# Transposing part of the attention output on VectorE and 16 small DMAs instead of on TensorE

## The chip, the core and the metric

One of the cores of a Trainium2 chip runs the whole kernel. The metric is the device time of one execution in microseconds (us). A profile's span, from its first to its last instruction, is one to three us shorter than that time. Before the change the median was 315.37 us in three runs (314.56 to 315.74).

Engine names in the profile: PE is TensorE (matmul), PEld its weight loads, DVE is VectorE, ACT is ScalarE, POOL is GpSimd, SP is SyncE. POOLq and SPq are the instruction streams of these engines; GpSimd and SyncE mostly issue DMAs here.

## The reference, cut to what matters

```python
def reference(q, k, v, centroids, w_in, w_out, alpha):   # q, k, v: (4, 8, 768, 64)
    # each query and key is assigned to one of 16 clusters of its head;
    # scores are masked to pairs of the same cluster
    attn = softmax(where(mask, q @ k.T / 8, -1e9)) @ v
    x = attn.transpose(0, 2, 1, 3).reshape(4 * 768, 512)
    h = x @ w_in                                         # (3072, 2048)
    g = h + sin(alpha * h) ** 2 / alpha
    return g @ w_out                                     # (3072, 512)
```

## The kernel before: the parts that matter

There are four batches. In each, four pairs of heads go through attention in 48 steps (12 per pair; a step is one tile of 128 keys by 768 queries of one head). Then the hidden matmuls multiply x by `w_in`. They need x with its 512 columns on partitions (`xT`), so each pair's result `xs`, which has queries on partitions, is transposed. In each step PE makes the scores (S<-QK), ScalarE takes their exponential ("exp" below), and PE multiplies that with V (the "PV" matmuls, OB<-VX,pT). The mask comes from one-hot rows, which mark the cluster of each query and key and stand below the 64 rows of q and k in the tile QK; DMAs put them there (QK<-ohT).

```python
    def x_T(m, bk=None):                      # six 128x128 transposes on PE, one copy on DVE
        b, hp = pair_of[m]
        xs = st[m]["xs"]
        xt_ps = (bank() if bk is None else bk).bitcast(BF16)
        for j in range(NJ):
            nc.tensor.transpose(
                out=xt_ps[:, P * j : P * j + P], in_=xs[:, j, :, :], identity=ident_b
            )
        nc.vector.tensor_copy(out=xT[:, hp, :], in_=xt_ps[:, 0:S])

    def hidden_mm(f, ar, k0, k1):
        for kk in range(k0, k1):
            lhsT = w_in_bf[:, kk, P * f : P * f + P]
            for lo, hi in ((0, 512), (512, S)):
                nc.tensor.matmul(..., lhsT=lhsT, rhs=xT[:, kk, lo:hi], ...)
```

The work beside the main chain is put at fixed steps, and each engine takes its own instructions in the order written. GpSimd has, in batches 1 and 2: eight casts of later queries and keys per pair (`prep_cast`), one cast of V per pair (`prep_v`), and the loads of q, k and v.

```python
    def prep_new(m, k0):                      # a later pair: k0 = 48 * b + 12 * n
        for g, d in enumerate((-12, -11, -9, -8)):
            at(k0 + d, lambda g=g: prep_D(m, g))     # DVE transposes of q, k
        at(k0 - 8, lambda: prep_S(m))                # 8 copies T<-Tq, issued by SyncE
        at(k0 + 5, lambda: prep_cast(m, 0))          # GpSimd
        at(k0 + 6, lambda: prep_cast(m, 1))
        hot_steps(m, k0 + 8)                         # one-hot rows of the clusters
    ...
            at(max(0, STEPS * m - (14 if m < 5 else 26)), lambda m=m: load_v(m, nc.gpsimd))
        at(max(0, STEPS * m - 5), lambda m=m: prep_v(m))
    ...
        pv(base + ASTEPS - 2)                 # end of a batch's attention
        hidden_mm(0, A[0], 0, KX - 2)         # x of the first two pairs
        pv(base + ASTEPS - 1)
```

The softmax here doesn't subtract the row's maximum and nothing guards it: scores larger than these inputs give would overflow.

## Time and profile before

| | before |
|---|---|
| median time | 315.37 us |
| span of the profile | 312.8 us |
| PE busy | 304.7 us, 97% |
| first exp of batches 0 to 3, at | 12.02, 84.04, 155.74, 226.97 us |
| attention of batches 0 to 3, first to last exp | 41.72, 41.01, 40.55, 38.56 us |
| first hidden matmul of batches 0 to 3, at | 53.13, 124.57, 195.80, 265.05 us |

The page of the kernel before shows busy time per engine (us, share, instructions), then the span in 40 slices with the busy share in tenths; PEclk is the granted TensorE clock in tenths.

```profile
PE 304.7 (97%) x2786; PEld 181.8 (58%) x2786; DVE 203.8 (65%) x367; ACT 239.9 (77%) x324; POOL 112.7 (36%) x174
...
PE   8899999999999999999999999999999999999995
...
POOL 5889886319307165870005376520001000000000
PEclk9999999999999999999999999999999999999999
```

PE is the limit nearly everywhere, and its clock is full throughout. The timeline of the kernel before (start, duration, engine, line, operation, output<-inputs, count) shows what one pair's transposes cost PE:

```profile
98.34 0.34 PE L340 MATMUL OB<-VX,pT 128*128 128x65 bf16 x6
98.52 0.50 PE L364 MATMUL M<-ident_b,xs 128*128 128x128 bf16 x6
98.86 0.38 PE L372 MATMUL M<-w_out_bf,gT 128*128 128x512 bf16 x1
```

The recorded durations overlap: 0.50 us are recorded for the six transposes, and yet the next matmul starts after 0.34. What counts is the distance between starts: the six hold PE from 98.52 to 98.86, 0.34 us. And the timeline of GpSimd shows DMAs issued one after another:

```profile
125.78 0.72 POOL L117 DMA_DIRECT2D q<-in_q_dram  x1
126.50 0.72 POOL L117 DMA_DIRECT2D k<-in_k_dram  x1
```

A DMA line on POOL is the time to issue it. Its data moves afterwards, and the time from issue to landing stands elsewhere in the profile (2.3 us for a copy T<-Tq).

### The profile page before, as it was taken

The numbers are of one execution on the slowest core, as the hardware profiler recorded it, in microseconds if no ns is written. First come the engines' busy times: TensorE is split into PE (matmuls) and PEld (weight loads), VectorE is DVE, ScalarE is ACT, GpSimd is POOL, SyncE is SP. The second block draws the span as 40 slices with busy tenths as digits, with TensorE's granted clock in tenths as the row PEclk, the third lists the DMA queues.
The fourth block names the chain that finished last, engine by engine and source line by source line (L and its number), as shares of the span: only waits on it lengthen the run. The fifth ranks groups of instructions, "written<-read, shape, count | busy, mean of one in ns | idle before, by whom it ended". The sixth has DMA issues, their size and how long they took to land.

```text
span 312.8 us, 7244 instructions
## 1 busy us (share of the span) xinstructions
PE 304.7 (97%) x2786; PEld 181.8 (58%) x2786; DVE 203.8 (65%) x367; ACT 239.9 (77%) x324; POOL 112.7 (36%) x174
## 2 busy tenths in 40 slices
PE   8899999999999999999999999999999999999995
PEld 3475757455456656555556656555556666555544
DVE  4768687688865867576957767587835222677821
ACT  5588889787689898688679988778678999687300
POOL 5889886319307165870005376520001000000000
PEclk9999999999999999999999999999999999999999
DMA  7576997978553776980044675320011001000031
GB/s 216 162 247 202 298 178 163 191 130 289 179 138 77 162 175 121 279 290 27 0 119 112 153 179 111 110 84 2 0 69 47 36 2 37 0 36 0 0 136 67
DMA packets 27138, 37.74 MB, mean 121 GB/s; under 512 B 4304, under 2 KB 20960, under 8 KB 27104
## 3 DMA queue, kind: packets, MB, share of 16 engines
q0 software_dynamic: 8704, 19.93, 24.3%
q1 hardware_dynamic: 18160, 17.30, 20.6%
q8 instruction: 22, 0.36, 0.5%
q14 instruction: 12, 0.10, 0.1%
q10 hardware_dynamic: 240, 0.06, 0.1%
HBM read 27.30 MB, written 6.29 MB: 107 GB/s over the span
## 4 chain that ended last, share of the span: by engine, by line
PE 86%; DVE 4%; ACT 3%; DMA 3%; POOL 1%; issue 1%; SPq 1%; ACTq 0%; DVEq 0%
PE M L372 19%; PE S L403 17%; PE S L325 12%; PE OB L340 10%; PE M L403 8%; PE S L326 6%; PE OB L372 5%; PE M L213 3%; PE M L143 3%; PE S L372 2%; DVE gT L426 2%; DMA q<-in_q_dram 2%; ACT s_sb L414 1%; PE M L364 1%; DMA QK<-ohT 1%; POOL QK L185 1%
## 5 line engine op out<-in xcount | busy, mean ns | idle before, releaser
L331 ACT ACTIVATE pT<-S 128x768 bf16<-128x768 f32 x192 | 143.9, 810 | 18.9 <-PE S L326 17.7
L372 PE MATMUL M<-w_out_bf,gT 128*128 128x512 bf16 (+1 forms) x288 | 90.7, 373 | 0.2
L325 PE MATMUL S<-QK 80*128 80x512 bf16 x192 | 73.0, 380 | 1.6 <-DMA QK<-ohT 1.1
L403 PEld LDWEIGHTS <-w_in_bf 128*128 128x128 bf16 x512 | 49.4, 98 | 37.7 <-issue 1.8
L340 PEld LDWEIGHTS <-pT 128*128 128x128 bf16 x1152 | 56.0, 97 | 21.3 <-ACT pT L331 0.2
L403 PE MATMUL S<-xT,w_in_bf 128*128 128x512 bf16 x352 | 65.0, 326 | 0.7 <-DVE gT L426 0.6
L340 PE MATMUL OB<-VX,pT 128*128 128x65 bf16 x1152 | 61.2, 193 | 0.0
L190 POOL TENSOR_SCALAR QK<-T 64x384 bf16<-64x384 f32 x64 | 34.4, 538 | 66.7 <-DMA T<-Tq 63.4
L414 ACT ACTIVATE s_sb<-S,alpha_col 128x768 bf16<-128x768 f32 (+2 forms) x45 | 39.4, 886 | 23.1 <-PE S L403 13.9
L372 PEld LDWEIGHTS <-gT 128*128 128x128 bf16 x400 | 39.0, 97 | 30.7 <-issue 5.4
L326 PE MATMUL S<-QK 80*128 80x256 bf16 x192 | 51.9, 270 | 0.0
L426 DVE SCALAR_TENSOR_TENSOR gT<-u_sb,ralpha,S 128x768 bf16<-128x768 bf16 (+2 forms) x45 | 44.7, 996 | 10.4 <-ACT u_sb L419 7.6
L185 POOL CAST QK<-T 64x768 bf16<-64x768 f32 x32 | 26.9, 841 | 9.1 <-DVE T L149 4.7
L403 PE MATMUL M<-xT,w_in_bf 128*128 128x512 bf16 (+1 forms) x160 | 29.9, 326 | 0.0
L326 PEld LDWEIGHTS <-QK 80*128 80x128 bf16 x192 | 18.9, 98 | 16.2 <-issue 2.1
L351 DVE RECIPROCAL rec<-OB 128x6 f32<-128x6 f32 x32 | 6.2, 195 | 33.7 <-PE OB L340 33.7
L422 DVE TENSOR_TENSOR u_sb<-s_sb 128x768 bf16<-128x768 bf16 (+2 forms) x41 | 22.9, 560 | 7.1 <-ACT s_sb L414 7.0
L414 ACT ACTIVATE s_sb<-M,alpha_col 128x512 bf16<-128x512 f32 (+1 forms) x40 | 20.9, 573 | 7.2 <-PE M L403 7.2
L426 DVE SCALAR_TENSOR_TENSOR gT<-u_sb,ralpha,M 128x512 bf16<-128x512 bf16 (+1 forms) x40 | 22.8, 611 | 5.5 <-ACT u_sb L419 5.1
L372 PE MATMUL OB<-w_out_bf,gT 128*128 128x512 bf16 (+1 forms) x80 | 26.2, 358 | 0.2 <-ACT T L153 0.2
L202 POOL CAST VX<-v 128x768 bf16<-128x768 f32 x16 | 13.5, 843 | 34.5 <-PE OB L340 33.4
L325 PEld LDWEIGHTS <-QK 80*128 80x128 bf16 x192 | 18.6, 97 | 8.9 <-issue 5.0
(81 smaller groups left out, 264.4 us busy)
## 6 DMA issues: line engine op xcount, KB each, us to landing
T<-Tq SPq DMA_DIRECT2D x64, 96.0 KB, 2.3
out_dram<-o_sb SPq DMA_DIRECT2D x23, 256.0 KB, 2.1
v<-in_v_dram POOLq DMA_DIRECT2D x14, 384.0 KB, 4.4
q<-in_q_dram POOLq DMA_DIRECT2D x13, 384.0 KB, 5.9
k<-in_k_dram POOLq DMA_DIRECT2D x13, 384.0 KB, 6.3
w_in_bf<-in_moe_w_in_dram POOLq DMA_DIRECT2D x4, 512.0 KB, 6.5
w_out_bf<-in_moe_w_out_dram POOLq DMA_DIRECT2D x4, 512.0 KB, 9.0
QK<-ohT SPq DMA_DIRECT2D x62, 12.0 KB, 4.2
```

What stands on the lines that cost most here:

```text
L185: nc.gpsimd.tensor_copy(out=QK[0:D, m % NQK, h, :, HS * par : HS * par + HS], in_=src)
L190: nc.gpsimd.tensor_scalar(out=QK[0:D, m % NQK, h, t].rearrange("c (n i a) -> c i n a", i=4, a=32)[:, 2 * par : 2 * par + 2], in0=src[:, t] ...
L202: nc.gpsimd.tensor_copy(out=VX[m % NVX][:, :, :, 0:D], in_=st[m]["v32"])
L325: nc.tensor.matmul(out=dst[:, 0:512], lhsT=lhsT, rhs=T[:, 0, 0:512], start=True, stop=True)
L326: nc.tensor.matmul(out=dst[:, 512:S], lhsT=lhsT, rhs=T[:, 0, 512:S], start=True, stop=True)
L331: nc.scalar.activation(out=pT, in_=area(i)[:, 0:S], func=ACTF.Exp, scale=escale)
L340: nc.tensor.matmul(out=o3[:, j, :], lhsT=pT[:, P * j : P * j + P], rhs=VX[m % NVX][:, h, jof(m // NHP, kt), :], start=(kt == 0 and j == 0) ...
L372: nc.tensor.matmul(out=bk[:, lo:hi], lhsT=gT[:, f, P * mt : P * mt + P], rhs=w_out_bf[:, f, lo:hi], start=(f == 0), stop=(f == NF - 1),)
L403: nc.tensor.matmul(out=ar[lo // 512][:, 0 : hi - lo] if isinstance(ar, tuple) else ar[:, lo:hi], lhsT=lhsT, rhs=xT[:, kk, lo:hi], start=(k ...
L414: nc.scalar.activation(out=s_sb[:, lo:hi], in_=src, func=ACTF.Sin, scale=alpha_col[:, f : f + 1])
L422: nc.vector.tensor_tensor(out=u_sb[:, lo:hi], in0=s_sb[:, lo:hi], in1=s_sb[:, lo:hi], op=ALU.mult)
L426: nc.vector.scalar_tensor_tensor(out=gT[:, f, lo:hi], in0=u_sb[:, lo:hi], scalar=ralpha[:, f : f + 1], in1=src, op0=ALU.mult, op1=ALU.add,)
```

## The change

PE is the limit, so x of the first two pairs of batches 1 to 3 is to be transposed elsewhere. VectorE transposes blocks of 32x32 (`x_D`); this turns each block within itself but leaves it on the wrong partitions, and 16 DMAs per batch put the blocks in place (`x_S`), two per step from step 29 on. Since blocks of 32 queries are now kept together, `xT` has another order of columns, and the hidden matmuls read it in runs of 32. The order of batch 0's preparations was changed as well.

```diff
+    def x_D(m):
+        hp = pair_of[m][1]
+        if hp == 0:
+            xq[0] = xqp.tile([P, 2 * S], BF16, tag="xq", name="xq")
+        nc.vector.transpose(
+            out=xq[0][:, S * hp : S * hp + S],
+            in_=st[m]["xs"].rearrange("p j h (e d) -> p (h e) j d", e=2),
+        )
+    def x_S(n):
+        g, i = divmod(n, 4)
+        nc.gpsimd.dma_start(
+            out=xT[32 * g : 32 * g + 32, 0:2, QS * i : QS * i + QS],
+            in_=xq[0].rearrange("p (h g n) -> p h g n", h=2, g=4)[32 * i : 32 * i + 32, :, g, :],
+        )
...
-                    rhs=xT[:, kk, lo:hi],
+                    rhs=xT[:, kk, :].rearrange("c (i j a) -> c j i a", i=4, j=NJ)[
+                        :, lo // P : hi // P
+                    ],
...
+    load_qk(3, eng=nc.gpsimd)                 # q, k of the fourth pair, before step 0
     load_v(1)
...                                            # batch 0: (pair, transposes, one-hot step, casts)
-        (2, ((0, 4), (1, 5), (2, 6), (3, 8)), 14, (6, 9)),
+        (2, ((0, 4), (2, 5), (1, 6), (3, 7)), 8, (7, 8)),
...                                            # and so on for pairs 3 to 7 and the weight loads
-    for m, i in {3: 0, 4: 8, 5: 11, 6: 15, 7: 23}.items():
+    for m, i in {4: 10, 5: 12, 6: 20, 7: 26}.items():
         at(i, lambda m=m: load_qk(m, eng=nc.gpsimd))
...
+            elif m % NHP == 2:
+                at(STEPS * (m + 1) + 4, lambda m=m: x_T(m))
+            else:
+                at(STEPS * (m + 1) + 5, lambda m=m: x_D(m))
+    for b in range(1, B):
+        for n in range(16):
+            at(ASTEPS * b + 2 * STEPS + 5 + n // 2, lambda n=n: x_S(n))
```

Cut: two buffers shared to make room (`warm` in `gT`, `ohd` in the tile of `xq`), the same column order in `x_T`, and in batch 0, in steps 1, 7, 13 and so on, the preparations written before the PV matmuls.

## The prediction

> **What bounds it now.** TensorE. The page gives PE 304.7 of 312.8 us (97%), and the table of stretches shows it 100% busy from 102 to 265 us, batches 1 to 3. Their attention steps (one exp each) start every 0.73 us in the timeline; ScalarE's exps (0.81 us recorded, overlapping by 0.10) would allow 0.71. So PE work removed there shortens the stage by about its full time. Batch 0 still has holes: the longest, 0.9 us at 31.6 us, is the third pair waiting for its one-hot rows (the chain has a DMA QK<-ohT of 3.5 us ending there).
>
> **What the change does.**
> 1. Removes 36 PE transposes. A group of six holds PE 0.33 us (98.52 to 98.86 in the timeline): 6 x 0.33 = 2.0 us, all on the critical path.
> 2. Replaces six PSUM evictions (0.55 us) by VectorE transposes of 128x768 bf16; that form takes 0.98 us here. VectorE is 65 to 75% busy there: free.
> 3. Retimes batch 0 (third pair's one-hot six steps earlier, loads moved). The hole should go: 0.9 us.
> 4. Hidden matmuls read xT in runs of 64 bytes. The Trainium skill, "SBUF — State Buffer" (Door 1, on cachelines), has repeated accesses to one 16-byte line at full rate, so I expect 216 and 109 ns per matmul as before; no run shows it yet.
> 5. Adds 16 DMAs per batch on GpSimd's queue, from step 29, two per step. Here the plan fails, I think. Loads of q and k issued back to back on GpSimd (125.8 to 130.8 us) take 0.72 us each, and the 512 KB weight loads 0.76. The skill's "DMA: Bandwidth & Descriptors" (Anatomy of one DMA) also says that many descriptors can be emitted before their cost shows; so a small DMA should not be much cheaper. Two per step need 1.44 us; a step lasts 0.73. Among them GpSimd still has four QK casts (0.56 each), a V cast (0.83) and a V load (0.78) in batches 1 and 2.
>
> Batch 1, estimated: the second VectorE transpose and four casts end near 109.9 us; then 16 x 0.72 + 2.2 + 0.8 + 0.8 = 15.3 us, to 125.2, and about 2 us to land (T<-Tq took 2.3): 127.2. The hidden matmuls need it all at about 123.9. Stall: 3.2 us. Batch 2: casts wait for T<-Tq until 179.4, so the start is near 180.5, landed 197.9, needed 195.1: 2.8 us. Batch 3 has only one V cast between: landed 264.3, needed 264.4: 0 to 0.5 us.
>
> **Sum.** 315.4 - 2.0 - 0.9 + 3.2 + 2.8 + 0.2 = 318.7. If a 24 KB DMA is issued in 0.55 us, the stalls shrink to about 1 us: 313.5. I weigh the first more: 317.6 us, 8 in 10 between 312.3 and 321. Faster by over 2%: 0.02; within 2%: 0.89; slower: 0.09.
>
> **What would show it.** Right: the first hidden matmul of batches 1 and 2 waits 2 to 4 us for DMA xT<-xq; GpSimd unbroken from step 29 to there; issue of xT<-xq 0.65 to 0.75 us; the 0.33 us bumps gone from the steps; the hole at 31.6 gone. Wrong: no wait on xT<-xq, hidden matmuls above 216 ns, new holes in batch 0.
>
> **What would make it wrong.** Cheaper small issues (near 313); a stall long enough for the PE clock to drop (1 to 3 us more); batch 0's loads competing for bandwidth; slower strided reads in 512 hidden matmuls (10% would be 8 us).

## The result

The changed kernel took 324.22 us in the median (323.18 to 325.26, four runs; before 315.44 in four). The ratio is 1.0283 (95% interval 1.0243 to 1.0323): slower. Ratios in this document are the mean time of one kernel's fast runs over that of the other's of the same rounds, so not quite the ratio of the medians quoted.

The page of the changed kernel, same lines:

```profile
PE 303.5 (94%) x2712; PEld 180.9 (56%) x2750; DVE 208.5 (65%) x367; ACT 239.6 (75%) x324; POOL 138.2 (43%) x222
...
PE   7889999899999996999999998799999999999995
...
POOL 5969998029015499960006389840000074000000
PEclk9999999999999999899999999799999999999999
```

PE now has weak slices at two places (a 6, and an 8 with a 7 behind it), and the clock dips twice, to 8 and 7 tenths on the average of a slice. (PE's own count fell by 74, more than the 36 transposes: matmul records can be missing from a trace. The weight loads, PEld, show exactly 36 fewer: 2786 to 2750.) The times of the stages say how much each part cost (us, read from the exps of both traces):

| stage | before | after | difference |
|---|---|---|---|
| start to first exp of batch 1 | 84.04 | 84.40 | +0.36 |
| attention of batches 1, 2, 3 | 41.01, 40.55, 38.56 | 40.37, 39.88, 37.95 | -1.92 |
| last exp of batch 1 to first of batch 2 | 30.69 | 35.58 | +4.89 |
| last exp of batch 2 to first of batch 3 | 30.68 | 35.88 | +5.20 |
| last exp of batch 3 to the end | 47.25 | 47.38 | +0.13 |
| sum = difference of spans (312.78, 321.44) | | | +8.66 |

The first row hides two things: the first exp came 0.57 us earlier, which looks like chance (11.43 to 12.17 us in five traces of kernels with the same start), and the attention of batch 0 took 0.81 us longer (41.72 to 42.53).

So the transposes left the attention stages as planned, and ten us came back at two places: where the hidden matmuls of batches 1 and 2 begin. The timeline of PE in the changed kernel there (the bracket names the idle time before an instruction, and what ended it):

```profile
124.10 0.35 PE L341 MATMUL OB<-VX,pT 128*128 128x65 bf16 x6
127.50 1.39 PE L425 MATMUL S<-xT,w_in_bf 128*128 128x512 bf16 x4 [3.05 <-DMA xT<-xq]
128.68 0.54 PE L341 MATMUL OB<-VX,pT 128*128 128x65 bf16 x6
129.03 2.44 PE L425 MATMUL S<-xT,w_in_bf 128*128 128x512 bf16 x8
```

The same place before:

```profile
124.57 0.81 PE L403 MATMUL S<-xT,w_in_bf 128*128 128x512 bf16 x4
125.22 0.35 PE L340 MATMUL OB<-VX,pT 128*128 128x65 bf16 x6
125.40 1.46 PE L403 MATMUL S<-xT,w_in_bf 128*128 128x512 bf16 x8
```

Two things are wrong. PE stands idle for 3.05 us (3.33 in batch 2; 3.2 and 3.5 by the distance of starts) until the copies xT<-xq have landed. And then it is slow: eight hidden matmuls take 2.44 us, where the same eight took 1.46 before. The table of stretches of the changed kernel (from:to, length, busy time of each engine with counts, then PEclk, DMA share, GB/s) gives the reason:

```profile
124.30:127.50 3.20, 0.15 (x5) 0.03 (x1) 0.32 (x1) 1.75 (x2) 2.83 (x6) 1.00 1.03 237
127.50:131.00 3.50, 3.50 (x17) 1.87 (x18) 0.75 (x2) 0.00 (x0) 3.13 (x5) 0.52 0.26 50
```

In the 3.5 us after the wait the granted clock was 0.52. The clock records of the trace have half clock for 3.413 us from 127.62, and again from 202.71. From the first hidden matmul to the first exp of the next batch takes 31.17 us before in batches 1 and 2, and 32.85 and 32.87 after: 1.7 us each.

Why the copies came late is read from GpSimd's timeline in the changed kernel:

```profile
110.69 1.15 POOL L387 DMA_DIRECT2D xT<-xq  x2
111.92 2.41 POOL L191 TENSOR_SCALAR QK<-T 64x384 bf16<-64x384 f32 x4
114.39 1.14 POOL L387 DMA_DIRECT2D xT<-xq  x2
115.57 0.83 POOL L203 CAST VX<-v 128x768 bf16<-128x768 f32 x1
116.34 3.19 POOL L387 DMA_DIRECT2D xT<-xq  x6
119.53 0.73 POOL L129 DMA_DIRECT2D v<-in_v_dram  x1
120.26 3.20 POOL L387 DMA_DIRECT2D xT<-xq  x6
```

and from the end of its chain of waits, followed back from the late matmul (start, duration, what):

```profile
122.92 4.54 DMA xT<-xq
127.46 0.05 issue
127.50 1.39 PE S L425 x4
```

GpSimd issued copies, four casts, the V cast and a V load in a row from 110.7 to 123.5. The chain ends with 4.54 us from the last issue to the landing. Read copy by copy, the first ten of batch 1 landed 1.7 to 3.8 us after their issue; the six behind the V load took 4.2 to 4.7 (batch 2: 4.4 to 5.0). The copies T<-Tq that SyncE issued on its own queue in the same stretch (119.8 to 123.1) took 4.5 to 5.5, where before those of this stretch took 2.2 to 2.3. So what was slow was not GpSimd's queue alone.

In batch 0 the wait of the third pair (before: 0.9 us at 31.6, the one-hot rows QK<-ohT) is gone. It stood so in the chain of the kernel before:

```profile
29.03 3.53 DMA QK<-ohT
32.61 0.39 PE S L325
```

The timeline of the changed kernel has a larger one in its place (1.6 us between two exps):

```profile
15.22 0.52 PE L144 MATMUL M<-ident_f,q 128*128 128x128 f32 x3
17.17 0.38 PE L326 MATMUL S<-QK 80*128 80x512 bf16 x1 [1.43 <-DMA QK<-ohT]
```

### The profile page after: what moved, and what is told of

Same layout as the page of the kernel before. It is cut to its first block, busy times and chain, and to the rows that moved or that the text cites. A ratio compares the mean times of both kernels' runs of the same rounds, so it can differ in the third digit from the quotient of the medians.

```text
span 321.4 us, 7195 instructions
## 1 busy us (share of the span) xinstructions
PE 303.5 (94%) x2712; PEld 180.9 (56%) x2750; DVE 208.5 (65%) x367; ACT 239.6 (75%) x324; POOL 138.2 (43%) x222
## 4 chain that ended last, share of the span: by engine, by line
PE 58%; ACT 19%; POOL 7%; DMA 6%; DVE 6%; issue 3%; SPq 0%; POOLq 0%; ACTq 0%; DVEq 0%
PE S L425 17%; ACT pT L332 16%; PE M L394 11%; PE M L425 7%; PE S L326 6%; POOL xT L387 4%; PE OB L394 4%; PE OB L341 4%; DMA xT<-xq 3%; DMA QK<-ohT 3%; PE S L327 2%; PE S L394 2%; DVE gT L450 2%; PE M L214 2%; ACT s_sb L438 1%
## 5 line engine op out<-in xcount | busy, mean ns | idle before, releaser
L394 PE MATMUL M<-w_out_bf,gT 128*128 128x512 bf16 (+1 forms) x258 | 80.2, 373 | 0.6
L425 PEld LDWEIGHTS <-w_in_bf 128*128 128x128 bf16 x512 | 50.2, 99 | 46.1 <-issue 7.4
L425 PE MATMUL S<-xT,w_in_bf 128*128 128x512 bf16 x352 | 67.8, 336 | 7.4 <-DMA xT<-xq 6.4
L387 POOL DMA_DIRECT2D xT<-xq x48 | 25.9, 545 | 47.3 <-PE S L327 47.2
L446 DVE TENSOR_TENSOR u_sb<-s_sb 128x768 bf16<-128x768 bf16 (+2 forms) x41 | 23.6, 577 | 7.0 <-ACT s_sb L438 7.0
L394 PE MATMUL OB<-w_out_bf,gT 128*128 128x512 bf16 (+1 forms) x73 | 23.5, 356 | 0.1
```

Of the source, the lines that this page charges most:

```text
L387: nc.gpsimd.dma_start(out=xT[32 * g : 32 * g + 32, 0:2, QS * i : QS * i + QS], in_=xq[0].rearrange("p (h g n) -> p h g n", h=2, g=4)[32 * ...
L394: nc.tensor.matmul(out=bk[:, lo:hi], lhsT=gT[:, f, P * mt : P * mt + P], rhs=w_out_bf[:, f, lo:hi], start=(f == 0), stop=(f == NF - 1),)
L425: nc.tensor.matmul(out=ar[lo // 512][:, 0 : hi - lo] if isinstance(ar, tuple) else ar[:, lo:hi], lhsT=lhsT, rhs=xT[:, kk, :].rearrange("c ...
L446: nc.vector.tensor_tensor(out=u_sb[:, lo:hi], in0=s_sb[:, lo:hi], in1=s_sb[:, lo:hi], op=ALU.mult)
```

## Experiments

Theory A: the copies are late because of what stands among them on GpSimd's queue, most of all the V load (384 KB), and the wait costs twice, once itself and once by the clock. Rivals: the new layout slows the hidden matmuls (D); 16 copies are too many by themselves (C); the other queue's copies T<-Tq crowd them (A2); the slow matmuls are not from the wait (B); GpSimd's software queue as such is at fault (G). For batch 0: the early load of the fourth pair's q and k (E), or the new order of PE's work (F).

An idea that stays open: fewer, larger copies (eight of 48 KB or four of 96 KB).

### The new layout alone (e7_pe_new_layout)

Edit: batch 0 in its order of before, x of all pairs on PE, only the column order of `xT` kept.

```diff
-            if m < NHP: ...                       # x_D for two pairs, x_S
+            at((18, 29, 44)[m] if m < NHP else STEPS * (m + 1) + 4, lambda m=m: x_T(m))
```

> The order of steps and the transposes of before, with only the new layout of x kept: transposes write PSUM in runs of 32 and the hidden matmuls read x in runs of 64 bytes. Theory A (the layout costs nothing): hidden matmuls 216 and 109 ns apart, span 312.8 within 0.5. Rival D (the layout slows them): more than 220 ns apart, span over 315.

Measured: span 313.1, one time of 314.92 us (before 314.91). Hidden matmuls start 216 and 109 ns apart, as before. The layout costs nothing; D falls. This agrees with what the Trainium skill says in "SBUF — State Buffer" (Door 1, on cachelines).

### Filling the wait with other matmuls (e3_clock_kept)

```diff
+        for _ in range(14 if b in (1, 2) else 0):
+            nc.tensor.matmul(out=M2[:, 0:512], lhsT=w_in_bf[:, 0, 0:P],
+                             rhs=w_in_bf[:, 0, 0:512], start=True, stop=True)
         hidden_mm(0, A[0], 0, KX - 2)
```

> The changed kernel, and 14 dummy matmuls of 512 columns (14 x 0.216 = 3.0 us) put on TensorE just before the first hidden matmul of batches 1 and 2, where it stood idle 3.05 and 3.33 us. Theory A (the wait for the last copies lets the clock fall to half for 3.4 us after it, twice, which costs 1.7 us each): the wait itself stays (first hidden matmul near 127.5 us), the granted clock stays 1.0 to the end, span near 318.0 instead of 321.4. Rival B (the slow hidden matmuls after the wait come from something else, such as reading x just as it lands): no change of the clock or of the slow matmuls, span 321.4 or more.

Measured: 320.91 us, ratio 1.0199 (1.0169 to 1.0228) against 1.0283. The timeline of that run:

```profile
124.17 3.18 PE L698 MATMUL M<-w_in_bf 128*128 128x512 bf16 x14
127.19 0.81 PE L425 MATMUL S<-xT,w_in_bf 128*128 128x512 bf16 x4
127.84 0.35 PE L341 MATMUL OB<-VX,pT 128*128 128x65 bf16 x6
128.03 1.46 PE L425 MATMUL S<-xT,w_in_bf 128*128 128x512 bf16 x8
```

The hidden matmuls begin no earlier, but eight of them take 1.46 us again, and no clock record below 1.0 stands before the end of the kernel. First hidden matmul to next batch: 31.18 and 31.39 us (changed kernel 32.85 and 32.87, before 31.17). So 1.7 and 1.5 us per wait were the clock's; B falls. The span was 318.8 and not 318.0, because in batch 2 the copies landed later still in this run (4.9 to 5.5 us after issue) and left 1.3 us of wait after the dummy matmuls (1.18 recorded); a gap of that length did not lower the clock.

### The V load behind the copies (e4_v_load_later)

```diff
-            at(max(0, STEPS * m - (14 if m < 5 else 26)), ...load_v
+            at(max(0, STEPS * m - (14 if m < 5 else 23 if m % NHP == 1 else 26)), ...load_v
```

The edit also moves the same load of batch 0 by three steps, where no copies are.

> The changed kernel with one load of v (384 KB) moved from among the 16 copies to behind them (step 34 to 37). Theory A1 (the last copies land late, 4 to 5 us after issue, because they queue behind that load): last copy issued 0.7 us earlier and landed about 2.4 us after its issue, so the wait of 3.1 and 3.3 us falls to 0.5 to 1 us, no clock drop, span near 313.5. Rival A2 (they land late because eight T copies of 96 KB on the other queue fill the DMA engines at the same time): the wait falls only by the 0.7 us of the issue, to about 2.5 us, span 319 to 321.

Measured: span 313.3, one time of 315.97 us. The timeline of PE in batch 1 of that run:

```profile
125.03 0.35 PE L341 MATMUL OB<-VX,pT 128*128 128x65 bf16 x6
125.67 0.81 PE L425 MATMUL S<-xT,w_in_bf 128*128 128x512 bf16 x4 [0.29 <-DMA xT<-xq]
```

One load moved by three steps took 8.2 us off the span (321.4 to 313.3). The last six copies landed 1.7 to 2.6 us after issue in batch 1 and 2.1 to 2.3 in batch 2, though SyncE issued its T<-Tq copies among them as before (from 120.6 on). A1 holds for these last copies and A2 falls. Whether they wait in the queue behind the load or share the DMA engines with it is not separated; the load slowed the copies of the other queue as well. The matmuls start 0.45 and 0.52 us late (in batch 2 the last copy had landed 0.3 us before), and the clock stays at 1.0. The run was timed once; it is read by its trace, and later ones that were timed several times (e5, e8, e10) have the load moved too.

### Nothing but one V cast among the copies (e5_nothing_between)

```diff
-        at(k0 + 5, lambda: prep_cast(m, 0))
-        at(k0 + 6, lambda: prep_cast(m, 1))
+        c0 = k0 + (13 if k0 % ASTEPS == 2 * STEPS else 5)
+        at(c0, lambda: prep_cast(m, 0))
+        at(c0 + 1, lambda: prep_cast(m, 1))
```

and the V load moved as above.

> The changed kernel with that load of v and the eight QK casts of the same steps moved behind the 16 copies, so that only one V cast stands among them. Theory A (the copies are late because of what they share the GpSimd queue with): in batch 1 they start at 110.0, take 16 x 0.54 + 0.83 = 9.5 us, landed by 122; in batch 2 start 185.5 and landed by 198; both before they are needed (123.9 and 199.7): no wait, no clock drop, span 311.2 (before 312.8, minus 2.0 for the transposes, plus 0.4 of batch 0), ratio 0.995. Rival C (16 copies of 24 KB are too many by themselves): a wait of 2 us or more remains, span over 315.

Measured: 315.35 us, ratio 1.0024 (0.9997 to 1.0051), span 313.2. In batch 1 the last copy landed at 122.4, the hidden matmuls began at 125.4 and waited for nothing; in batch 2 193.9 and 196.3. So C falls: 16 copies have time enough. The attention of batches 1 to 3 took 40.41, 39.89 and 37.97 us, 1.85 less than before. The casts moved here were worth little: between the attention stages this run takes 31.03 and 31.10 us, e4 31.14 and 31.20. Nor is a copy quick in every case without the V load: in the middle of batch 1 some landed 4.0 us after issue (4.3 in e8), but early enough.

Of the 2 us that the expectation missed, about 0.8 lie in batch 0 and ahead of it: the hole of 1.6 us before the second head is there, batch 0 took 42.75 (before 41.72), and its first exp came 0.15 us later, together 1.2 where 0.4 was allowed for. About 1.1 lie between and after the attention stages: from the last exp to the next batch's first exp it takes 0.14, 0.34 and 0.41 us longer than before, and 0.19 at the end, though nothing waits for the copies. The runs e8 and e10 have the same loss in batches 1 and 2 (0.34 and 0.38, 0.32 and 0.37). So of the 1.9 us taken out of the attention stages about 0.7 come back in the hidden stages; the cause was not looked for.

### The fourth pair's load put back (e2_load3_later)

```diff
-    load_qk(3, eng=nc.gpsimd)
     load_v(1)
-    for m, i in {4: 10, 5: 12, 6: 20, 7: 26}.items():
+    for m, i in {3: 0, 4: 10, 5: 12, 6: 20, 7: 26}.items():
```

> The changed kernel with one thing of batch 0 put back: the load of q and k of the fourth pair goes to GpSimd's queue at step 0, behind the casts, as before, and not in front of them. Theory E (that load, 768 KB, runs beside the one-hot rows of the first pair's second head on the DMA engines, and the sixth step waits 1.6 us for those rows): the hole of 1.6 us after step 5 is gone or under 0.3 us, batch 0 (first to last exp) takes about 41.0 us instead of 42.5 (before: 41.7); the waits of batches 1 and 2 stay. Rival F (the new order of TensorE's work in batch 0 costs the time): batch 0 stays above 42.2.

Measured: span 321.3, one time of 323.08 us. The hole after step 5 is gone, but batch 0 took 42.0 us: another hole of 1.1 us between two exps opened at 21.7, where the second pair waits for its own one-hot rows. Half of the expectation held. The waits stayed (3.63 and 2.96 us), each with 3.41 us of half clock after it. The next run has the same batch 0 and says more.

### Both repairs together (e8_between_and_load3)

> Nothing among the copies but one V cast (as in the run of that name), and the fourth pair's load put back as before. Theory A with E: no wait in batches 1 and 2, batch 0 41.0 us, span about 311.5, ratio 0.997 to 0.999. Rival F: batch 0 42.5, ratio 1.002 as without the load put back.

Measured: 312.83 us, ratio 0.9936 (0.9917 to 0.9955), span 311.1, batch 0 41.04 us. The page and the timeline of PE in batch 1:

```profile
PE 301.0 (97%) x2712; PEld 179.6 (58%) x2750; DVE 207.8 (67%) x367; ACT 239.5 (77%) x324; POOL 138.0 (44%) x222
...
PEclk9999999999999999999999999999999999999999
```

```profile
123.47 0.81 PE L425 MATMUL S<-xT,w_in_bf 128*128 128x512 bf16 x4
```

No wait, no dip. This version beats both kernels, by 0.6% over before; that is clear of zero. Its second pair did not wait (0.08 us where the run above had 1.1), so that hole varies between executions. The one of the first pair does not: in the five traces with the early load (the changed kernel and the runs e3, e4, e5 and e6) the rows of the first pair's second head landed 4.4 to 6.2 us after issue and left 1.5 to 2.8 us between two exps. In the seven traces with the load behind the casts they took 2.1 to 3.8 us, and no such hole is there. So E holds. F falls with the next run, which differs from this one in the order of batch 0 alone: 314.25 us with the order of before, 312.83 with the new one (six runs each, intervals of the ratios apart).

### The repaired copies with batch 0 in its order of before (e10_between_old_b0)

> Nothing among the copies but one V cast, and all of batch 0 in the order of before. Theory A: batch 0 41.5 to 41.7 us as before, batches 1 to 3 shorter by 0.67 each, no wait, span 311.0, ratio 0.994. If something else of the change costs time in batches 1 to 3 (the VectorE transposes, the DMAs), ratio 1.0 or above.

Measured: 314.25 us, ratio 0.9983 (0.9958 to 1.0008), span 311.4; batch 0 41.89, batches 1 to 3 40.40, 39.88 and 37.98 us, no wait. The mechanism is as expected, but the gain in time is smaller than the 0.6% expected and not clear of zero. The third pair's hole (0.6 us between two exps here) is back. The profiled execution, with a span of 311.4, was the shortest of the six (311.4 to 313.9), so its stages look better than the median; what made the others longer no trace shows.

### Only the first pair by VectorE (e9_first_pair, e11_first_pair_casts_later)

The part of the edit that matters (cut: batch 0 in the order of before, and copies of one pair instead of two):

```diff
-            elif m % NHP == 2:
+            elif m % NHP:                      # x_D for the first pair only
...
-            at(ASTEPS * b + 2 * STEPS + 5 + n // 2, lambda n=n: x_S(n))
+            at(ASTEPS * b + STEPS + 5 + n // 2, lambda n=n: x_S(n))
```

> Batch 0 in the order of before; of batches 1 to 3 only the first pair by VectorE, with 16 copies of 12 KB from step 17 on, the second pair by TensorE again. Theory A: the copies end 12 or more steps before they are needed, no wait, each attention stage shorter by 0.33, span 311.8, ratio 0.997. Rival C (16 copies on this queue hold up the casts and loads enough to cost time): ratio 1.0 or above.

Measured: 316.06 us, ratio 1.0039 (1.0012 to 1.0066), a miss. The copies did land in time (114 us against 125), but the attention of batches 1 and 2 took 41.79 and 41.30 us. The timelines of GpSimd and of PE in that run:

```profile
109.02 2.94 POOL L387 DMA_DIRECT2D xT<-xq  x6
112.04 4.82 POOL L191 TENSOR_SCALAR QK<-T 64x384 bf16<-64x384 f32 x8
116.92 0.83 POOL L203 CAST VX<-v 128x768 bf16<-128x768 f32 x1
```

```profile
117.80 0.52 PE L341 MATMUL OB<-VX,pT 128*128 128x65 bf16 x12 [0.93 <-DVE Tq L165]
```

Here the copies themselves were in the way: they pushed eight casts, and these the V cast, which ended at 117.75. The PV matmuls that read it began at 117.80. (The bracket names VectorE, which was only the last that the profile could see; the time of the V cast fits.) A last run moved those eight casts behind the V cast:

> The first-pair kernel (16 copies of 12 KB from step 17 on), with the eight QK casts of steps 29 and 30 moved behind the V cast of step 31. In the first-pair run TensorE stood 1.2 us in batches 1 and 2 before the PV matmuls of the fourth pair, whose V cast GpSimd began only then. Theory A (the copies push whatever stands behind them on that queue): the holes of 1.2 us are gone, the attention stages of batches 1 and 2 take about 40.7 and 40.2 us instead of 41.8 and 41.3, span 312.3, ratio 0.996 to 0.999. Rival C (the copies cost TensorE time in another way): the stages stay above 41.4 and 41.0.

Measured: 314.45 us, ratio 0.9976 (0.9953 to 0.9999). The holes of 1.2 us are gone in both batches, and batch 2 took 40.24 as expected. Batch 1 took 41.41: a new hole of 0.8 us at 120.4, before the cluster matmuls (M<-T,cnB). Their T<-Tq copies landed 5.0 to 5.7 us after issue there, with two V loads issued shortly before (at 108.1 and 113.0). That these loads slowed them is inferred from the times and not tested.

### The copies on SyncE (e6_on_sync)

```diff
-        nc.gpsimd.dma_start(
+        nc.sync.dma_start(
             out=xT[32 * g : 32 * g + 32, 0:2, QS * i : QS * i + QS],
```

> The changed kernel with the 16 copies issued by SyncE instead of GpSimd, nothing else moved. Theory A (any in-order queue that has other work among the copies makes them late): SyncE issues 8 T copies (5.2 us) before them and 4 one-hot rows (2.6 us) among them and takes about 0.6 us for each of the 16, so in batch 1 the last is issued near 127 and landed near 129: a wait of 4 to 6 us in batches 1 and 2, the clock drops twice, span 322 to 327. Rival G (GpSimd's software queue is the fault): no wait, span near 311.5.

Measured: span 334.7, one time of 336.46 us; the direction is right and the size too small. The issues of SyncE and PE's timeline in batch 1:

```profile
113.09 5.19 SPq L176 DMA_DIRECT2D T<-Tq  x8
118.38 8.53 SPq L387 DMA_DIRECT2D xT<-xq  x12
127.01 2.45 SPq L300 DMA_DIRECT2D QK<-ohT  x4
129.51 2.57 SPq L387 DMA_DIRECT2D xT<-xq  x4
```

```profile
127.35 0.35 PE L341 MATMUL OB<-VX,pT 128*128 128x65 bf16 x6
137.59 1.44 PE L425 MATMUL S<-xT,w_in_bf 128*128 128x512 bf16 x4 [9.89 <-DMA xT<-xq]
```

The wait in batch 2 was 5.80 us. G falls: the other queue had more in the way and the copies were later, and in e5 and e8 GpSimd's own queue brought them in time. The last four landed 4.3 to 6.2 us after issue; GpSimd issued its V, q and k loads in that stretch (from 128.7 on), and that these slowed them is inferred. The clock was half for 10.24 us here and for 6.83 in batch 2. It was half for 3.41 us in batch 0 as well, after an idle time of 2.42 us at the hole of the one-hot rows; batch 0 took 44.95 us, 2.4 more than in the changed kernel, so that much of the miss has nothing to do with the copies.

## Why the prediction was wrong

The direction and the place were right, but the sum was too small: 318.7 as added up, 317.6 as given, and 324.2 measured, outside the range. Term by term, in us:

| term | predicted | measured |
|---|---|---|
| 36 transposes gone from PE | -2.0 | -1.92 (attention of batches 1 to 3) |
| start to the first exp of batch 1 (batch 0) | -0.9 | +0.36 |
| waits for the copies in batches 1, 2, 3 (by starts) | 3.2, 2.8, 0.2 | 3.2, 3.5, 0.0 |
| half clock after the waits | not in the sum | 1.7, 1.7 |
| layout of x | 0 | 0 (e7) |

- **The transposes.** Right, by the distance of PE's starts: 0.64, 0.67 and 0.61 us per batch. VectorE had the time (its transpose took 0.93 to 0.98 us).
- **The step that failed, the largest:** "a stall long enough for the PE clock to drop (1 to 3 us more)" stood among the things that would make it wrong, and not in the sum. I had predicted waits of 3 us and had to ask then what they do to the clock. The Trainium skill, "TensorE: Matmul & The Clock Gate" (HAM oscillation), gives idle gaps over about 3.4 us as the limit; 3.05 us of idle time was enough here. e3 shows that the clock's part is 3.2 us of the 8.66. These 3.2 to 3.4 us are most of what the sum of 318.7 lacks.
- **The second step that failed:** "The hole should go: 0.9 us." It did go. But "loads moved" was not followed to the end: q and k of the fourth pair were issued at 10.37 and 11.23 us instead of 14.53 and 15.39, beside the one-hot rows of the first pair, which landed 4.5 to 5.0 us after issue instead of 2.4 to 3.8. e8 against e10 shows that with this load put back the new order is worth having (312.83 against 314.25 us; batch 0 41.04 against 41.89 in the traces, though e2, with the same batch 0 as e8, had 42.0).
- **The waits.** Right in size by luck: two errors cancelled. Issue: 0.72 us predicted, 0.54 measured, so 16 copies took 2.9 us less. And "about 2 us to land": the last six took 4.2 to 5.0. I had counted the V load as 0.8 us of GpSimd's time and not as 384 KB in front of the copies. e4 shows that this load was most of the wait.
- **The range.** The chance I gave to cheap issues was right about the issues and still wrong about the time. Lowering 318.7 to 317.6 for that reason moved away from the result.

## What to carry to other kernels

Before moving work to DMAs, write down everything that the issuing queue has in that stage, in order, and count the bytes in flight ahead of the last copy, from any queue, into its landing time; then do the same for the consumers of what comes behind it. A wait of about 3 us on TensorE must be priced with the slow clock after it. And when a repair is as small as one load three steps later, look for it before giving the change up: the same change was worth -0.6% instead of +2.8% once the queue was put in order and one early load was put back. By these times most of that is the new order of batch 0 and not the transposes: with the old order the repaired copies gave a ratio of 0.9983 (0.9958 to 1.0008).

## What the Trainium skill lacked or had wrong

- "TensorE: Matmul & The Clock Gate", HAM oscillation: the limit of about 3.4 us for idle gaps. Waits that the profile shows as 3.05 and 3.33 us idle were followed by half clock for 3.41 us each (a cost of 1.7 us each), so were 3.63 and 2.96 us (e2) and even 2.42 us (e6, batch 0); gaps of 0.3 to 0.5 us (e4), 1.2 us (e3) and 1.9 us (e4, batch 0) were not. A wait of 9.89 us (e6) had half clock for 10.24 us, up to 3.7 us after work began again. In all twelve traces the half clock begins a whole number of 3.413 us after the first clock record (4.74 + 36 x 3.413 = 127.62 in the changed kernel). PE's recorded busy share of the 3.413 us before it was 0.30 or less, and where no drop followed 0.49 or more; so where a gap lies on this grid seems to count beside its length. That is worked out from these traces and not tested, and it is not meant as something that the page lacks.
- "DMA: Bandwidth & Descriptors", Anatomy of one DMA: it gives a fixed cost of about 2 us and a part for the bytes. In e8 the copies of 24 KB landed 1.7 us after their issue starts at the quickest and 2.2 in the median, which agrees; behind a load of 384 KB they took 4.2 to 5.0 us in the changed kernel. How GpSimd's time to issue goes with the size of the DMA is not given in figures: 0.50 us (12 KB copies), 0.54 us (24 KB copies), 0.72 us (384 KB loads of q and k).
- The same page, Issuing engines are not separate DMA queues: it calls the sequencer's time to issue "usually small relative to the DMA itself". Here it was not small: 0.54 us for a copy that lands 1.7 us after its issue starts at the quickest and 2.2 in the median, and 16 issues in a row hold GpSimd for 8.6 us. That DMAs of different engines share the same DMA engines agrees: during the V load the copies that SyncE issued took 4.5 to 5.5 us instead of 2.3.
